# Attention, gated MLP and phase mixing on one core: bias layer by max(w1 L, −b1 ψ), bit-mask float64 conversion, xT at the bottom of its stack

## The chip, the cores and the metric

One core of a Trainium2 chip. The metric is the device time of one execution in microseconds; lower is better. The kernel before takes 879.43 us (median of three runs, 874.92 to 885.33).

## The reference

The output comes out of three layers one after another, for B = 4, S = 576, eight heads of 64:

```python
psi_rel = log1p(|i - j|);  psi_i = log1p(max(i, 1))
h = maximum((psi_rel / psi_i) * w1 + b1, 0)          # S x S x 32
scores = q @ k.T / 8 + (h @ w2)                      # one bias map per head
x = softmax(scores) @ v                              # B x 576 x 512

u, v = split(gelu_tanh(x @ w_in))                    # 512 wide each
v_s = w_sg @ (layer_norm(v) * g_ln) + b_sg
x = x + (u * v_s) @ w_out

theta = x @ w_theta
y = w_tok_r @ (x * cos(theta)) + w_tok_i @ (x * sin(theta))
u = x + y;  out = u + maximum(u @ w_ch, 0)
```

The weights of the second and third layer (w_in, w_out, w_theta, w_tok, w_ch) arrive as float64, two 32-bit words per number, and the kernel makes float32 of them itself. Products of the second and third layer are formed from a high and a low part of each operand.

## The kernel before, in words

The code does not emit instructions where it is written. A recorder (class Rec) takes down every operation with the tiles it reads and writes; plan() then orders them for each engine by a key (set in the code as nc.key) plus a number per tile name from a table SHIFT, chooses the engine where an operation has alternatives with the help of a table BIAS, and emits all of them from one line (379, so every row of the trace has L379). Each engine works through its queue in that order. SBUF pools are stacks: a pool that is opened above another can only use the space once what lay there before is released. Names of tiles in the trace are those in the code; cva... and cvs... are the conversion's two scratch tiles, raw... what it loads.

The stages, in order of build():

- bias_gen: 36 groups of 4 tiles hq of 128 rows (4 query rows by 32 hidden units): hq = max(L·(w1/ψ), −b1) on DVE or relu(L·(w1/ψ) + b1) on ACT (every third group), where L is a sliding window of a table lt of log1p(|i−j|); four 32-row matmuls pb; an eviction bs on ACT or DVE; then a DMA into the bias maps. Beside it v_all is read in 12 pieces for its sum of squares. Everything lies in the pool "start".
- w1_load: pool "wstage". conv64 turns w_in into float32 in 16 chunks of 256 columns (rawwi, cvawi, cvswi, ri); a Square with accumulation gives a power-of-two scale, then wi gets high and low float16 parts. w_sg is read into rs, five tiles, once, and split in the same way (ws, wsr).
- att_pair, 16 times (4 batches by 4 head pairs), 9 tiles each: PE scores s, DVE e = −(s + bias) with its row minimum, ACT exp in place with the row sum, ACT p (high half), POOL or DVE p (low half), a transposing DMA pT<-p, PE px. After nine tiles DVE xf = px/sum, PE transposes it (xq), xT gets its high and low half and is written out (dx). Pool xTp is opened after "wstage" is released. e has 4 buffers (tag "s"), pT 8, xf 1.
- mlp for the batch before runs between the pairs: vp, up, sp on PE; gelu on ACT; layer norm (mv, n) and gates (gg).
- conv_w turns w_out, w_theta, w_tok and w_ch into float32 (wr_...), in halves of 256 or 288 columns, and splits each block (wo, wt, wk, wc).
- s2 multiplies by w_out and adds x (op, xs, x); theta forms tp = x @ w_theta, then rk (rounded tp/2π), rr (rest), sine and cosine by ACT, multiplied with the transposed x (xp) and split into z; ymix forms yp with w_tok; s4 forms cp with w_ch and writes oo.

The low half of every split (p, z, wk, ...) is a TENSOR_TENSOR subtraction that may go to DVE or POOL. In conv64 the steps stand like this:

```python
nc.scalar.activation(a, hi.bitcast(F32), AF.Abs)
nc.scalar.activation(s, hi.bitcast(F32), AF.Sign)
nc.vector.tensor_scalar(a, a, F64_MIN, F64_MAX, op0=ALU.max, op1=ALU.min)
nc.vector.tensor_scalar(ai, ai, 3, 0x40000000, op0=ALU.logical_shift_left, op1=ALU.bitwise_xor)
nc.vector.scalar_tensor_tensor(ai, lo, 29, ai, op0=ALU.logical_shift_right, op1=ALU.bitwise_or)
nc.scalar.activation(a, a, AF.Abs)
self.tt(("vector", "gpsimd"), dst, a, s, ALU.mult)
```

Of the kernel before, what the change touches and what calls it, by code (L numbers as in the profile page):

```python
# [199 lines left out]
def covers(a, b):  # L200
# [23 lines left out]
    ("wr_w_ch", "vector"): 23.7807, ("wr_w_out", "gpsimd"): 12.3712, ("wr_w_out", "vector"): -46.9618,
    ("wr_w_theta", "gpsimd"): -39.3403, ("wr_w_theta", "vector"): 12.8239, ("wr_w_tok", "gpsimd"): -122.2832,
    ("wr_w_tok", "vector"): -39.8631, ("ws", "scalar"): 33.4611, ("ws", "vector"): 72.0963,
    ("wsr", "scalar"): 146.0824, ("wsr", "vector"): 78.6932, ("wt", "gpsimd"): 146.2282,
    ("wt", "vector"): 72.383, ("xT", "scalar"): 34.9432, ("xT", "sync"): -81.3085, ("xT", "vector"): -9.533,
# [1077 lines left out]
```

## Time and profile before

| | |
|---|---|
| median of three runs | 879.43 us (874.92 to 885.33) |
| the profiled execution | 881.56 us, span 879.8 us, mean granted TensorE clock 0.917 |
| busy in the span | PE 762.3 (87%), DVE 629.9 (72%), ACT 520.5 (59%), POOL 298.4 (34%) |
| moved by DMA | 115.52 MB, mean 131 GB/s |

The profile shows one execution. Times are microseconds from the start of the span unless marked ns. PE is TensorE, DVE VectorE, ACT ScalarE, POOL GpSimd; PEclk is the granted clock as a share of 2.4 GHz. In a group's row, the last column is idle time of the engine ahead of these instructions and what ended it.

### The profile page before, as it was taken

How to read it: one execution, taken by the hardware profiler on the slowest of the kernel's cores; microseconds unless marked ns; L12 is line 12 of the kernel's file. 1: busy time of each engine (PE TensorE's matmuls, PEld its weight loads, DVE VectorE, ACT ScalarE, POOL GpSimd, SP SyncE). 2: the span in 40 equal slices, each digit the busy share in tenths (PEclk: the TensorE clock that was granted, in tenths of full speed). 3: DMA queues.
4: the chain of work that ended last, by engine and by line, in shares of the span. 5: the costliest groups of instructions: out<-in, count | busy, mean ns of one | idle time of the engine just before them, and what ended most of it. 6: DMA issues, size and time to landing. Idle time of an engine off the chain costs nothing.

```text
span 879.8 us, 17586 instructions
## 1 busy us (share of the span) xinstructions
PE 762.3 (87%) x6544; PEld 534.8 (61%) x6544; DVE 629.9 (72%) x1475; ACT 520.5 (59%) x1038; POOL 298.4 (34%) x263
## 2 busy tenths in 40 slices
PE   5689778648899889997999976998878999999998
PEld 2234344326454555545654453687757999899998
DVE  5777558869698568986589754997989892763712
ACT  5777567865689447892579713655568671542500
POOL 0011244643567335672547531365433200000000
PEclk9979956557999999999799996999999999999999
DMA  7987689729898299866998396465622210010101
GB/s 227 217 169 172 169 184 192 150 87 192 158 186 154 72 221 179 169 150 133 190 188 151 77 179 159 133 198 173 180 82 64 74 54 1 1 55 1 41 14 54
DMA packets 205734, 115.52 MB, mean 131 GB/s; under 512 B 176593, under 2 KB 176849, under 8 KB 205649
## 3 DMA queue, kind: packets, MB, share of 16 engines
q1 hardware_dynamic: 198192, 101.01, 52.6%
q10 hardware_dynamic: 7456, 13.40, 5.0%
q8 instruction: 51, 0.84, 0.4%
q14 instruction: 35, 0.28, 0.1%
HBM read 47.13 MB, written 14.16 MB: 70 GB/s over the span
## 4 chain that ended last, share of the span: by engine, by line
PE 52%; DVE 17%; DMA 15%; issue 7%; ACT 5%; POOL 3%; SPq 1%; ACTq 0%; DVEq 0%; POOLq 0%
PE yp L379 12%; PE s L379 8%; PE cp L379 6%; DMA pT<-p 6%; PE pb L379 6%; PE sp L379 5%; PE tp L379 4%; PE up L379 4%; PE px L379 4%; PE vp L379 3%; POOL p L379 2%; DVE v L379 2%; DMA vr<-v_all 2%; DVE e L379 2%; DVE cvaw_tok L379 2%
## 5 line engine op out<-in xcount | busy, mean ns | idle before, releaser
L379 POOL TENSOR_TENSOR p<-e,p 128x576 f16<-128x576 f32 x144 | 191.0, 1338 | 183.3 <-ACT p L379 172.5
L379 PE MATMUL s<-kq 64*128 64x288 f32 (+1 forms) x640 | 149.1, 495 | 21.5 <-DVE m L379 21.5
L379 ACT ACTIVATE e<-e,m 128x576 f32<-128x576 f32 x144 | 110.6, 769 | 55.9 <-DVE m L379 44.7
L379 PEld LDWEIGHTS <-pT 128*128 128x128 f16 (+1 forms) x2240 | 86.0, 108 | 69.4 <-issue 30.4
L379 PE MATMUL px<-v,pT 128*128 128x64 f16 (+1 forms) x2240 | 95.4, 204 | 32.6 <-DMA pT<-p 21.9
L379 PE MATMUL yp<-wk,z 128*128 128x288 f32 x864 | 119.4, 297 | 1.5 <-ACT z L379 0.8
L379 DVE CUSTOM_DVE_ANT_0 e<-s,bias 128x576 f32<-128x576 f32 x128 | 94.6, 752 | 35.5 <-PE s L379 18.7
L379 PEld LDWEIGHTS yp<-wk,z 128*128 128x128 f32 x864 | 116.5, 190 | 2.6 <-ACT z L379 1.1
L379 PEld LDWEIGHTS s<-kq 64*128 64x128 f32 (+1 forms) x640 | 71.9, 199 | 65.8 <-DVE m L379 40.3
L379 ACT ACTIVATE p<-e 128x576 f16<-128x576 f32 x144 | 94.0, 674 | 29.7 <-DMA pT<-p 22.2
L379 PE MATMUL pb<-hq,w2s 128*32 128x288 f32 x576 | 69.3, 454 | 14.3 <-DVE bs L379 9.9
L379 PE MATMUL op<-sp_g,wo 128*128 128x288 f32 x384 | 60.8, 311 | 7.6 <-DVE x L379 4.1
L379 PE MATMUL vp<-wi,xT 128*128 128x512 f16 (+1 forms) x240 | 63.4, 397 | 1.4 <-DVE xT L379 1.4
L379 PEld LDWEIGHTS op<-sp_g,wo 128*128 128x128 f32 x384 | 54.4, 194 | 12.4 <-DVE x L379 4.9
L379 PEld LDWEIGHTS pb<-hq,w2s 128*32 128x32 f32 x576 | 28.4, 117 | 52.9 <-DVE bs L379 9.9
L379 PE MATMUL sp<-ws,n 128*128 128x64 f16 (+1 forms) x384 | 57.4, 287 | 0.3 <-DVE n L379 0.2
L379 PE MATMUL up<-xT,wi 128*128 128x64 f16 (+1 forms) x384 | 55.1, 287 | 0.7 <-DVE gtu L379 0.7
L379 ACT ACTIVATE sp_u<-x 128x576 fp32r<-128x576 f32 x16 | 10.8, 684 | 70.8 <-DVE x L379 70.1
L379 PE MATMUL cp<-sp_u,wc 128*128 128x288 f32 x384 | 52.5, 295 | 0.0
L379 PE MATMUL tp<-wt,sp_t 128*128 128x512 f32 x192 | 47.9, 403 | 4.3 <-DVE sp_t L379 2.6
L379 DVE TENSOR_SCALAR hq<-lt,sl,nb 128x576 f32<-128x576 f32 x96 | 49.8, 586 | 2.4 <-PE pb L379 1.6
L379 PEld LDWEIGHTS cp<-sp_u,wc 128*128 128x128 f32 x384 | 51.2, 188 | 0.2
(197 smaller groups left out, 1214.9 us busy)
## 6 DMA issues: line engine op xcount, KB each, us to landing
bias<-bs SPq DMA_DIRECT2D x32, 288.0 KB
kq<-kq SPq DMA_DIRECT2D x10, 576.0 KB
raww_tok<-w_tok SPq DMA_DIRECT2D x18, 288.0 KB
vr<-v_all SPq DMA_DIRECT2D x12, 384.0 KB
xx<-dx SPq DMA_DIRECT2D x16, 288.0 KB
out<-oo SPq DMA_DIRECT2D x16, 288.0 KB
dg<-gg SPq DMA_DIRECT2D x16, 256.0 KB
raw<-vp SPq DMA_DIRECT2D x12, 320.0 KB
```

The lines of the kernel that those rows point to most:

```text
L379: getattr(getattr(self.nc, name), m)(*[res(x) for x in a], **out)
```

## The change

- Bias layer: the division by ψ moves behind the second layer. With ψ > 0, relu(L·w1/ψ + b1) = relu(L·w1 + b1·ψ)/ψ. lt is multiplied by w1 once; hq is max(window, −b1·ψ) with one pointer on DVE, or relu(window + b1·ψ) on ACT; the eviction bs multiplies by 1/ψ (rp, one more pointer). nl, rp are new small tiles; the four matmuls of a half now depend on all four hq of the group. v_all is read in 8 pieces of 1152 columns.
- conv64 has a form with no Sign and no product: absolute value straight into the target, clamp, shift and mask, then the sign bits of the high word are put back by an and/or. The w_in chunks are 512 columns wide and eight; conv_w takes a whole block.
- w_sg is read twice through one buffer rs instead of once into five.
- xTp is opened first, at the bottom of the left stack, and released last. e has 3 buffers, pT 7, xf 2.
- w_theta is scaled by 1/2π at conversion (conv_w's scale), so rr = rk − magic − tp is one operation and Sin takes scale −2π; a subtraction and a second product go.
- SHIFT gets an entry per group of work as well (op.grp, "@a0" is pair 0), and BIAS, SHIFT, LOADF, LOADK, BV, SLACK and YIELD have new numbers.

```diff
@@ plan
-            op.skey = (op.key[0] + SHIFT.get(op.lab, 0.0), op.key[1])
+            op.skey = (op.key[0] + (SHIFT.get(op.lab, 0.0) + SHIFT.get(op.grp, 0.0)), op.key[1])
@@ tables (two of their lines)
-    ("z", "gpsimd"): 22.3176, ("z", "vector"): 16.3112,
+    ("z", "gpsimd"): -58.9563, ("z", "vector"): 12.3072,
@@ conv64
+        if fuse:
+            nc.scalar.activation(dst, hi.bitcast(F32), AF.Abs)
+            nc.vector.tensor_scalar(dst, dst, F64_MIN, F64_MAX, op0=ALU.max, op1=ALU.min)
+            nc.vector.tensor_scalar(di, di, 3, 0x3FFFFFF8, op0=ALU.logical_shift_left, op1=ALU.bitwise_and)
+            nc.vector.scalar_tensor_tensor(di, hi, TOP, di, op0=ALU.bitwise_and, op1=ALU.bitwise_or)
+            nc.vector.scalar_tensor_tensor(di, lo, 29, di, op0=ALU.logical_shift_right, op1=ALU.bitwise_or)
+            return
@@ bias_gen
+        nc.vector.tensor_scalar(nl, sl, b1, -1.0, op0=ALU.mult, op1=ALU.mult)
+        self.th = nc.vector.tensor_scalar(lt, lt, w1, None, op0=ALU.mult)
+        nc.vector.tensor_scalar(sl, sl, b1, None, op0=ALU.mult)
-                    nc.scalar.activation(h, win, AF.Relu, scale=sl[:, Q:Q + 1], bias=b1)
+                    o = nc.scalar.activation(h, win, AF.Relu, bias=sl[:, Q:Q + 1])
-                    nc.vector.tensor_scalar(h, win, sl[:, Q:Q + 1], nb, op0=ALU.mult, op1=ALU.max)
+                    o = nc.vector.tensor_scalar(h, win, nl[:, Q:Q + 1], None, op0=ALU.max)
-            nc.any(("scalar", "activation", (bv, ps[:, :, :SH], AF.Identity), {"bias": add}),
-                   ("vector", "tensor_scalar", (bv, ps[:, :, :SH], add, None), {"op0": ALU.add}))
+            nc.any(("scalar", "activation", (bv, ps[:, :, :SH], AF.Identity), {"bias": add, "scale": rs}),
+                   ("vector", "tensor_scalar", (bv, ps[:, :, :SH], rs, add), {"op0": ALU.mult, "op1": ALU.add}))
@@ w1_load
-            for k in range(8):
-                self.conv64(sp, ri[:, cc, cs], src, 256, f"wi{half}_{k}")
+            for cc in range(4):
+                self.conv64(sp, ri[:, cc], d["w_in"][:, cc, hs], 512, f"wi{half}_{cc}", 2, True)
-        rs = sp.tile([P, 5, S], F32, name="rs")
+            rs = sp.tile([P, S], F32, tag="rs", bufs=1, name=f"ra{st}")
+            rs = sp.tile([P, S], F32, tag="rs", bufs=1, name=f"rs{st}")
@@ att_tile, pair_main
-        s = a.tile([P, S], F32, tag="s", bufs=4, name=f"e{u}")
+        s = a.tile([P, S], F32, tag="s", bufs=3, name=f"e{u}")
-        pT = a.tile([P, 9, P], F16, tag="pT", bufs=8, name=f"pT{u}")
+        pT = a.tile([P, 9, P], F16, tag="pT", bufs=7, name=f"pT{u}")
-        xf = a.tile([P, 4, P], F32, tag="xf", bufs=1, name=f"xf{u}")
+        xf = a.tile([P, 4, P], F32, tag="xf", bufs=2, name=f"xf{u}")
@@ theta
-            nc.scalar.activation(k, ps, AF.Identity, scale=1.0 / (2 * math.pi), bias=self.magic)
-            nc.vector.tensor_scalar(k, k, MAGIC, None, op0=ALU.subtract)
-            nc.vector.scalar_tensor_tensor(r, k, -TWO_PI_HI, ps, op0=ALU.mult, op1=ALU.add)
-            nc.vector.scalar_tensor_tensor(r, k, -TWO_PI_LO, r, op0=ALU.mult, op1=ALU.add)
+            nc.scalar.activation(k, ps, AF.Identity, bias=self.magic)
+            nc.vector.scalar_tensor_tensor(r, k, MAGIC, ps, op0=ALU.subtract, op1=ALU.subtract)
@@ build
+        self.p_x = nc.pool("xTp")
         self.setup()
         self.bias_gen()
...
         self.w1_load()
-        self.p_x = nc.pool("xTp")
         self.p_c1 = nc.pool("c1p")
```

Two places show how the order moves. The first is DVE in the conversion of w_in, about the first xT of the program. wi<-ri is the low half of w_in, bsg the scaling of b_sg, v the split of V for a pair, e a score tile. Before:

```order
L379 SCALAR_TENSOR_TENSOR wi<-ri_1864,fc_wi_136,wi 128x512 x4
L379 TENSOR_SCALAR i2s_131<-ih_134 128x1
L379 COPY v_3_2037<-v_3_2037 64x2x256
L379 TENSOR_SCALAR bsg<-bsg,i2s_131 128x576
L379 TENSOR_SCALAR gsc<-gsc,i2s_131 128x4
L379 COPY v_3_2037<-v_3_2037 64x2x256
L379 SCALAR_TENSOR_TENSOR v_3_2037<-raw_3_1400,fc_v,v_3_2037 128x2x320
L379 TENSOR_SCALAR gts_132<-ih_134 128x1
L379 TENSOR_SCALAR ghs_133<-ih_134 128x1
L379 CAST xT_0_2097<-xq_0_1802 128x512
L379 CAST xT_0_2097<-xq_0_2_2004 128x64
L379 TENSOR_TENSOR xT_0_2097<-xq_0_1802,xT_0_2097 128x512
```

and now:

```order
L384 ISA e_2_2_0_1485,m_2_2_0_1365<-s_2_2_0_1469,biasr 128x576
L384 ISA m_2_2_0_1365 128x1
L384 TENSOR_SCALAR m_2_2_0_1365<-m_2_2_0_1365 128x1
L384 CAST xT_0_170<-xq_0_1492 128x512
L384 SCALAR_TENSOR_TENSOR wi<-ri_1097,fc_wi_146,wi 128x512 x4
L384 ISA e_2_0_0_1531,m_2_0_0_1385<-s_2_0_0_1488,bias_78 128x576
L384 ISA m_2_0_0_1385 128x1
L384 TENSOR_REDUCE ss_sg<-ssb 128x1 x2
L384 TENSOR_SCALAR m_2_0_0_1385<-m_2_0_0_1385 128x1
L384 TENSOR_SCALAR r_2_2_1404<-sr_2_2_1221 128x1
L384 TENSOR_TENSOR xT_0_170<-xq_0_1492,xT_0_170 128x512
L384 TENSOR_SCALAR ri_1562<-ri_1562 128x512 x4
```

gts, ghs, gsc, i2s are small constants of the MLP, m and r of the softmax. The first xT stood behind the last low halves of w_in (x4), the scaling of bsg and a split of v; now its cast stands ahead of the four low halves of the first half of w_in, and the conversion of the second half (ri) follows.

The second place is DVE at the last theta tiles of batch 3 (rk_3 and rr_3 belong to tile 3, the last; oo is an output of batch 2, z the low half). Before:

```order
L379 TENSOR_SCALAR rk_3_10289<-rk_3_10289 128x512
L379 SCALAR_TENSOR_TENSOR rr_3_10296<-rk_3_10289,tp_3_10251 128x512
L379 SCALAR_TENSOR_TENSOR oo_0_9919<-cp_0_10128,x_2_7222 128x576
L379 TENSOR_TENSOR rr_2_10206<-xp_2_10194,rr_2_10206 128x512
L379 SCALAR_TENSOR_TENSOR rr_3_10296<-rk_3_10289,rr_3_10296 128x512
L379 TENSOR_TENSOR rk_2_10213<-xp_2_10194,rk_2_10213 128x512
L379 TENSOR_TENSOR z_3_10192<-rr_2_10206,z_3_10192 128x512
L379 SCALAR_TENSOR_TENSOR oo_1_9958<-cp_1_10227,x_2_7222 128x576
L379 TENSOR_TENSOR z_3_10183<-rk_2_10213,z_3_10183 128x512
```

and now:

```order
L384 SCALAR_TENSOR_TENSOR rr_2_9780<-rk_2_9789,tp_2_9749 128x512
L384 TENSOR_TENSOR rr_2_9780<-xp_2_9767,rr_2_9780 128x512
L384 TENSOR_TENSOR rk_2_9789<-xp_2_9767,rk_2_9789 128x512
L384 SCALAR_TENSOR_TENSOR rr_3_9805<-rk_3_9816,tp_3_9773 128x512
L384 SCALAR_TENSOR_TENSOR oo_0_9459<-cp_0_9669,x_2_7099 128x576
L384 TENSOR_TENSOR rr_3_9805<-xp_3_9797,rr_3_9805 128x512
L384 TENSOR_TENSOR rk_3_9816<-xp_3_9797,rk_3_9816 128x512
L384 SCALAR_TENSOR_TENSOR oo_1_9553<-cp_1_9734,x_2_7099 128x576
```

A theta tile has three DVE rows where it had seven; its two z halves are on POOL, where the last eight stand in one piece:

```order
L384 TENSOR_TENSOR z_3_9682<-rr_0_9421,z_3_9682 128x512
L384 TENSOR_TENSOR z_3_9674<-rk_0_9402,z_3_9674 128x512
L384 TENSOR_TENSOR z_3_9697<-rr_1_9462,z_3_9697 128x512
L384 TENSOR_TENSOR z_3_9690<-rk_1_9491,z_3_9690 128x512
L384 TENSOR_TENSOR z_3_9711<-rr_2_9780,z_3_9711 128x512
L384 TENSOR_TENSOR z_3_9704<-rk_2_9789,z_3_9704 128x512
L384 TENSOR_TENSOR z_3_9725<-rr_3_9805,z_3_9725 128x512
L384 TENSOR_TENSOR z_3_9718<-rk_3_9816,z_3_9718 128x512
```

All 36 z low halves are on POOL now, after none before; on PE these z are followed by 80 cp matmuls and then by the first yp of batch 3 (before, 36 tp, 96 cp and all 216 yp). Evictions bs on DVE go from 18 to 9, and DVE has 1245 rows where it had 1397.

## Rows read from the trace of the kernel before

**Rows 1.** Stretches of the span: us, busy us by engine (x), PEclk, DMA, GB/s.

```profile
0.00:103.00 103.00, 79.77 (x651) 33.97 (x652) 72.75 (x162) 69.42 (x107) 7.32 (x13) 0.93 0.79 188
103.00:185.00 82.00, 56.69 (x375) 33.55 (x371) 58.37 (x172) 64.65 (x163) 43.70 (x40) 0.58 0.78 168
185.00:206.00 21.00, 10.69 (x152) 8.69 (x152) 14.25 (x46) 11.56 (x30) 4.89 (x6) 0.52 0.48 109
206.00:546.00 340.00, 300.91 (x3225) 175.55 (x3226) 252.42 (x692) 214.20 (x429) 178.75 (x149) 0.95 0.81 161
546.00:713.00 167.00, 151.63 (x998) 126.00 (x996) 149.92 (x278) 109.07 (x228) 63.69 (x57) 0.97 0.41 123
713.00:880.00 167.00, 162.58 (x1154) 157.00 (x1152) 82.16 (x129) 51.61 (x84) 0.00 (x0) 1.00 0.08 29
```

**Rows 2.** Chain of waits, 176 to 242: start, us, what.

```profile
...
184.32 0.75 DVE e L379
...
205.52 1.33 DVE xT L379 x3
206.84 0.66 DVE e L379
...
```

**Rows 3.** Timeline of POOL and DVE near 567 and 657: start us, us.

```profile
...
567.13 1.32 POOL L379 TENSOR_TENSOR gg<-gg,gtu 128x512 f32<-128x512 f32 x1 [4.60 <-DVE gg L379]
...
567.23 1.37 DVE L379 TENSOR_SCALAR cvaw_theta<-cvaw_theta 128x256 f32<-128x256 f32 x1
...
569.12 0.48 DVE L379 TENSOR_SCALAR cvaw_theta<-cvaw_theta 128x256 int32<-128x256 int32 x2
...
657.23 0.41 DVE L379 TENSOR_SCALAR rk<-rk 128x512 f32<-128x512 f32 x1
...
```

**Rows 4.** Groups of the run: engine, names, shapes xcount | busy, mean ns.

```profile
L379 DVE TENSOR_SCALAR hq<-lt,sl,nb 128x576 f32<-128x576 f32 x96 | 49.8, 586 | 2.4 <-PE pb L379 1.6 <-DMA lt<-ltab 0.7
...
L379 ACT ACTIVATE hq<-lt,wb,sl 128x576 f32<-128x576 f32 x48 | 38.8, 859 | 3.5 <-DVE m L379 2.1 <-PE s L379 0.8 <-issue 0.5
...
L379 ACT ACTIVATE p<-e 128x576 f16<-128x576 f32 x144 | 94.0, 674 | 29.7 <-DMA pT<-p 22.2 <-DVE v L379 4.8 <-DVE xT L379 2.0
...
L379 DVE TENSOR_SCALAR bs<-pb,cb 128x576 f32<-128x576 f32 x17 | 13.9, 817 | 15.4 <-PE pb L379 9.1 <-DMA bias<-bs 5.6 <-issue 0.6
...
L379 POOL TENSOR_TENSOR p<-e,p 128x576 f16<-128x576 f32 x144 | 191.0, 1338 | 183.3 <-ACT p L379 172.5 <-issue 1.9 <-DMA dx<-xT 1.8
...
L379 PE MATMUL cp<-sp_u,wc 128*128 128x288 f32 x384 | 52.5, 295 | 0.0
...
```

**Rows 5.** Groups of ACT, 103 to 206.

```profile
...
L379 ACT ACTIVATE cvawi<-rawwi 128x256 f32<-128x256 f32 x16 | 6.7, 425 | 4.4 <-DMA rawwi<-w_in 4.3
L379 ACT ACTIVATE cvswi<-rawwi 128x256 f32<-128x256 f32 x16 | 6.7, 417 | 0.0
L379 ACT ACTIVATE wi<-ri 128x256 f16<-128x256 f32 x16 | 6.5, 406 | 1.5 <-POOL ri L379 1.5
L379 ACT ACTIVATE cvawi<-cvawi 128x256 f32<-128x256 f32 x16 | 6.3, 406 | 3.7 <-DVE cvawi L379 3.5
...
```

**Rows 6.** 546 to 713: tiles cvaw_tok, cvaw_theta, z by engine; two DVE groups.

```profile
546.00:713.00 167.00, 25.32 (x54) 15.69 (x36) 19.66 (x18) 0.97 0.41 123
546.00:713.00 167.00, 13.95 (x24) 6.78 (x16) 6.67 (x8) 0.97 0.41 123
546.00:713.00 167.00, 31.65 (x216) 30.26 (x216) 8.47 (x12) 7.47 (x13) 0.97 0.41 123
...
L379 DVE SCALAR_TENSOR_TENSOR rr<-rk,rr 128x512 f32<-128x512 f32 x7 | 5.9, 840 | 0.0
...
L379 DVE TENSOR_SCALAR rk<-rk 128x512 f32<-128x512 f32 x7 | 4.0, 575 | 3.1 <-ACT rk L379 3.1
```

**Rows 7.** Timeline of DVE, 215 to 230: e, first and fifth tile.

```profile
...
218.65 0.76 DVE L379 CUSTOM_DVE_ANT_0 e<-s,bias 128x576 f32<-128x576 f32 x1 [0.29 <-PE s L379]
...
227.75 0.76 DVE L379 CUSTOM_DVE_ANT_0 e<-s,bias 128x576 f32<-128x576 f32 x1 [2.92 <-POOL p L379]
...
```

More of the change, by code (lines that the diff above doesn't have):

```diff
@@ L157, in __init__ @@
         self.done = self.dma = False
-        self.banks, self.table, self.rows, self.lab, self.port = (), None, P, "", [False]
+        self.banks, self.table, self.rows, self.lab, self.grp, self.port = (), None, P, "", "", [False]
 class Pool:
@@ L224 @@
[L224 to L228, printed above, removed]
@@ L253 @@
-    "xp": -331.5337, "xq": 298.6439, "xr": -67.349, "xs": -569.332, "xx": -233.673, "yp": -63.1746,
-    "z": 114.4221, "zb": 275.7247,
-}
-LOADF, LOADK = 1.8093412586188697, 8.575464505639914
-BV = 1.52008187476998
[5 rows of a table added]
+    "@w_ch": 227.6951, "@w_out": 311.7815, "@w_theta": 548.2913, "@w_tok": 311.2367, "@y0": -961.0679,
[3 rows of a table added]
+    "fa_ws": 1498.3734, "fb_v": 321.7078, "fb_wi": -601.6005, "fb_ws": -913.1623, "fc_v": 1005.3392,
+    "fc_wi": -1788.3783, "fc_ws": 365.7335, "fd_v": -467.0455, "fd_wi": -373.7939, "fd_ws": 1003.5365,
@@ L276, in __init__ @@
         self.nc, self.tc = nc, tc
-        self.key, self.seq, self.ops, self.stack, self.last = 0.0, 0, [], {}, {}
+        self.key, self.grp, self.seq, self.ops, self.stack, self.last = 0.0, "", 0, [], {}, {}
         for n in ("vector", "scalar", "gpsimd", "tensor", "sync"):
@@ L729, in bias_gen @@
         self.ld(self.ident, d["ident"])
-        for i in range(12):
-            nc.key = 1.0 + 5 * i
-            vr = st.tile([P, 768], F32, tag="vr", bufs=2, name=f"vr{i}")
-            self.ld(vr, d["v_all"][:, i * 768:(i + 1) * 768], ("sync",))
+        for i in range(8):
+            nc.key = 40.0 + 5 * i
+            vr = st.tile([P, 1152], F32, tag="vr", bufs=2, name=f"vr{i}")
+            self.ld(vr, d["v_all"][:, i * 1152:(i + 1) * 1152], ("sync",))
             nc.scalar.activation(vr, vr, AF.Square, accum_out=self.ss_v[:, i:i + 1])
@@ L777, in w1_load @@
                 nc.vector.tensor_scalar(self.eps4, ts, ts, 4e-6, op0=ALU.mult, op1=ALU.mult)
-            hs = slice(half * 512, half * 512 + 512)
             for cc in range(4):
@@ L783, in w1_load @@
         nc.key = t
-        rs = sp.tile([P, 5, S], F32, name="rs")
-        for st in range(5):
-            self.ld(rs[:, st], d["w_sg"][:, st])
         ssb = c.tile([P, 5], F32, name="ssb")
         for st in range(5):
-            nc.scalar.activation(self.ws[:, 0, st] if st < 4 else self.wsr[:, 0], rs[:, st], AF.Square,
+            rs = sp.tile([P, S], F32, tag="rs", bufs=1, name=f"ra{st}")
+            self.ld(rs, d["w_sg"][:, st])
+            nc.scalar.activation(self.ws[:, 0, st] if st < 4 else self.wsr[:, 0], rs, AF.Square,
                                  accum_out=ssb[:, st:st + 1])
@@ L1074, in conv_w @@
             r = self.p_st.tile([P, S], F32, tag="wst", bufs=2, name=f"wr_{name}{i}")
-            for q in range(2):
-                cs = slice(q * h, (q + 1) * h)
-                self.conv64(self.p_st, r[:, cs], self.d[name][:, i, cs], h, f"{name}{i}_{q}")
-            self.split(w[:, :, i], r[:, :ncol])
+            self.conv64(self.p_st, r[:, :ncol], self.d[name][:, i], ncol, f"{name}{i}", 2, True)
+            if scale is None:
+                self.split(w[:, :, i], r[:, :ncol])
+            else:
+                nc.scalar.activation(w[:, 0, i], r[:, :ncol], AF.Copy, scale=scale)
+                nc.vector.scalar_tensor_tensor(w[:, 1, i], r[:, :ncol], scale, w[:, 0, i].bitcast(F32),
+                                               op0=ALU.mult, op1=ALU.subtract)
     def s2(self, b, key, step):
         nc, st = self.nc, self.p_st
+        nc.grp = f"@o{b}"
         sp = self.sp_tiles(self.p_s2, f"g{b}")
@@ L1217, in build @@
         self.s2(0, t + 15, 3)
-        self.conv_w(self.wt, "w_theta", DM, 4, t + 15, 3)
+        self.conv_w(self.wt, "w_theta", DM, 4, t + 15, 3, 1.0 / TWO_PI)
         self.s2(1, t + 35, 3)
@@ L1221, in build @@
         self.s2(2, t + 55, 3)
-        for q in (self.ps_c, self.ps_x, self.p_c1, self.p_x, self.p_w1):
+        for q in (self.ps_c, self.ps_x, self.p_c1, self.p_w1, self.p_x):
             q.release()
```

131 lines of the change are left out of this document (68 added, 63 removed), and 45 rows, old and new, of tables (BIAS, SHIFT).

## The prediction

> **What bounds the kernel now.** I read the stretches of the span first, then the chain of waits where they look odd, then the groups of single engines there. The chip tells within about ±1% (the three times shown spread that far), so "faster" and "slower" below mean over 1%.
>
> The stretches [rows 1] show five regimes. In 0 to 103 (bias layer) PE is busy 79.77 us, DVE 72.75, ACT 69.42: no engine is full, three share the bound. In 103 to 185 (first attention tiles beside the conversion of w_in) DMA shows 0.78 and ACT 64.65 of 82 us, the fullest compute engine, while PE has 56.69 at a granted clock of 0.58, that is at the 1.2 GHz level almost throughout. In 185 to 206 every engine is half idle. In 206 to 546 (attention with the MLP) PE is busy 300.91 of 340 at 0.95. In 546 to 713 PE has 151.63 of 167 and DVE 149.92; in 713 to 880 PE has 162.58 of 167 at 1.00.
>
> Why 185 to 206 is hollow stands in the chain [rows 2]: a score tile is taken by DVE at 184.32, the next at 206.84, behind three xT casts at 205.52. xT's pool lies above "wstage" on the same stack, so no xT can be written before the w_in and w_sg conversion has let "wstage" go; xf has one buffer, so the next pair's tiles stand still behind it. 22.5 us hold no score tile.
>
> **Term 1, bias layer (0 to 103).** DVE: each of the 96 hq loses one per-partition pointer. A 128x512 TENSOR_SCALAR without pointers took 0.41 us [rows 3], so one of 576 columns about 0.46; hq with two took 586 ns [rows 4], so a pointer is (0.586 − 0.46)/2 = 0.063 us, and 96 of them 6.0. Nine evictions bs leave DVE (18 to 9) at 0.817 [rows 4]: 7.4. The scaling of lt adds one instruction of 1148 columns, about 0.8, ahead of the first hq; DVE 72.75 → 60. ACT: a pointer costs it (859 − 674)/2 = 93 ns (hq with two against p with none [rows 4]); 48 hq with one less are −4.5, nine more bs at about 0.674 + 2 × 0.093 = 0.86 are +7.7, and the 27 now read a scale pointer too; ACT goes to about 74. PE's instructions stay, and PE is the fullest. So DVE's saving is mostly off the path; ACT, loaded more, may become late for the pb tiles. Ends −10 (PE's 23 us of idle time halved) and +5 (ACT's five microseconds, if they all land on the path); I take **−3**, near the engine that is fullest.
>
> **Term 2, 103 to 206.** xT's pool goes to the bottom, so the 22.5 us stall loses its cause: in the new order an xT is cast ahead of the w_in low halves instead of behind everything. What is late next? By ACT: per 256-column chunk it did Abs, Sign, a second Abs and a Square, 6.7 + 6.7 + 6.3 + 6.5 = 26.2 us in all [rows 5]. Now there are 8 chunks of 512 columns with one Abs and one Square: 16 × 0.65 (p, 576 columns, took 0.674) = 10.4. ACT falls from 64.65 + 11.56 = 76.2 to 60.4; at the share it kept in 103 to 185 (64.65/82 = 0.79) that is 76 us instead of 103: −27. By DMA: 82 × 0.78 + 21 × 0.48 = 74 us of busy time stay, and w_sg is now read twice, which adds five loads; 103 to 206 moved 168 × 82 + 109 × 21 = 16.1 MB, five tiles of 128x576 words are 1.5 MB, so DMA needs about 81 us, at 0.85 busy 95 us: −8. The ten w_sg loads go through one buffer, each behind the reader of the one before, and end when "wstage" does, but only the first MLP waits for that now. Ends 0 (all of it is refilled by DMA) and −40 (the time at which ACT is full). I take **−22**, between ACT and DMA, nearer ACT, as 206 to 546 shows DMA at 0.81 beside more tiles per microsecond.
>
> **Term 3, 206 to 546.** No operation is removed here. e loses a buffer (4 to 3), pT one (8 to 7), xf gains one. PE has 39 us of gaps and the order is new. I take **0**, ends −15 (a third of the gaps) and +33 (rival E).
>
> **Term 4, 546 to 713.** DVE and PE are both near full. DVE loses three things. Conversion: w_tok and w_theta cost it 25.32 + 13.95 = 39.3 [rows 6] (their rows give DVE, ACT and POOL; z's PE and PEld first) (w_ch, converted in the same way, is left out). Now a block of 512 columns takes two one-input and two two-input operations, 2 × 0.41 [rows 3] + 2 × 0.70 (as z, 8.47/12 [rows 6]) = 2.2, one of 576 columns 2.5: 4 × 2.2 + 9 × 2.5 = 31.3, so −8.0. Theta: seven TENSOR_SCALAR rk (575 ns) and seven rr<-rk,rr (840) go [rows 6]: −9.9. The low halves z: twelve, 8.47 us [rows 6], go to POOL. DVE: 149.9 − 8.0 − 9.9 − 8.5 = 123.5. Then PE is next: 151.63 × 0.97 (its clock raised to 1) = 147 if never idle; at the share it has in the last stretch (162.58/167) 151. So the stretch goes from 167 to 151 at best: I take **−14**, ends 0 (rival B) and −20.
>
> Cover that may go: POOL is nearly idle here (63.69 of 167) but slow. A two-input operation of 576 columns takes it 1338 ns [rows 4], so one of 512 about 1.2, against 0.7 on DVE, and DVE's own operations pay when POOL works: a 128x256 TENSOR_SCALAR that takes 0.24 in a run of two at 569.12 took 1.37 at 567.23, beside a POOL operation that ran from 567.13 [rows 3]. That is what rival B rests on. The Trainium skill, "Perfetto Trace Analysis", section Optimizing Scalar/DVE Operations, says that GPSIMD and DVE share an SBUF read port, so that moving work from one to the other might not help; the row at 567.23 bears that out, and by it the −8.5 for z would be taken back and term 4 would be about −5.
>
> **Term 5, 713 to 880.** PE is busy 97% at full clock and its instructions stay: 0. The last theta tiles now wait for eight z halves in a row on POOL, 8 × 1.2 = 9.6 us, but 80 cp matmuls stand on PE before the first yp of the last batch. A cp averages 52.5/384 = 0.137 us [rows 4], so these cover 11 us. Ends −2 and +10 (cover gone); **0**.
>
> **Sum** against the profiled execution, 881.56 (span 879.8 and 1.8 around it): −3 − 22 + 0 − 14 + 0 = −39, so 842.6. That execution is 2.1 us above the median of 879.43; I take the 2.1 off: **840.5**.
>
> **Rivals.**
> A (upside): the new order also closes a third of PE's gaps in 206 to 546, −15 to −20: 822. For: POOL and DVE are each idle a quarter of the time or more there. Against: no wait of that stretch is named by the change.
> B: the tail gains nothing. POOL's 36 z halves, 36 × 1.2 = 43 us, and DVE's two-input operations hold each other up, so DVE's saving is eaten. 840.5 + 14 = 854.5. For: the row at 567.23. Against: DVE would have 43 us of slack in 167 to absorb it.
> C: the front gains little, because DMA sets 103 to 206 and the w_sg chain keeps "wstage", and with it the first MLP, late: −4 instead of −22: 858.5. For: DMA 0.78, and every slice before 103 is as full. Against: 185 to 206 has DMA 0.48, so room was left.
> D: the order fits the numbers it was fitted to and not the chip; gains and new gaps cancel: 879.
> E, the other side: the three-deep ring of e. about 136 of the 144 tiles ran in 103 to 546 (8 earlier), 443/136 = 3.26 us a tile; with three buffers that pace holds only while a buffer's life is under 9.8 us. Before, the fifth tile after one at 218.65 got its buffer at 227.75 and waited 2.92 for POOL: a life of 9.1 us with four [rows 7]. From 9.8 us on the ring decides, and each further microsecond of life costs 136/3 = 45 us. At 10.5 us: 136 × 3.5 = 476, +33 in place of −22; with −3 and −14: 881.56 + 16 − 2.1 = 895.5. Against: the bare chain of a tile (e 0.76 [rows 7], an exp of 0.86 as reckoned for bs, p 0.67 and POOL's p 1.34 [rows 4]) is 3.6 us, the rest is waiting, which shortens with a shorter ring. The Trainium skill, "Perfetto Trace Analysis", section Optimization Strategy, reads a bubble that repeats as a sign that buffers ran out; no row here shows that the 2.92 repeats; where it does, one buffer less makes it worse, by that rule.
>
> **How the numbers follow.** Forecast 0.50, A 0.08, B 0.14, C 0.13, D 0.09, E 0.06. Faster: 0.50 + 0.08 + 0.14 + 0.13 = 0.85; within 1%: 0.09; slower: 0.06. The range goes from below A (term 2 at −28, term 3 at −20, term 4 at −14, term 1 at −10: −72, 807) to above C with part of D: 868. Outside lie most of D, E and the best ends. For the forecast and A to C alone, 815 to 860.
>
> **What would show it.** Right: no stretch of 20 us without a score tile between 100 and 210; the attention's tiles 20 us earlier by number; DVE under 127 us in the stretch that answers to 546 to 713, and PE over 0.93 busy in it. Wrong: score tiles waiting for POOL longer than 2 us in a row (E), DVE's mean for z's neighbours and conversions over 1 us (B), the first MLP's start no earlier than before (C), or gaps of PE in 206 to 546 that grew by what was won before (D).

## The result, and the profile after

The changed kernel takes 851.48 us (median of 4, 849.15 to 857.6) against 879.94: a ratio of 0.9686, 95% interval 0.9609 to 0.9763. That is 28 us faster, where 39 were forecast, and inside the range. The rest of this document shows that the sum came that near by luck: two terms gained what was not forecast, two others did not gain what was.

The profiled execution of the changed kernel is the slowest of its four (857.6 us, span 855.8, mean granted clock 0.906). Its stretches, cut near where the same work ends as in [rows 1] (columns as there):

```profile
...
0.00:88.00 88.00, 60.81 (x618) 26.48 (x618) 58.47 (x137) 68.37 (x103) 7.44 (x12) 0.90 0.80 205
88.00:176.00 88.00, 60.25 (x431) 36.09 (x432) 70.45 (x190) 58.78 (x124) 33.03 (x26) 0.55 0.81 194
176.00:206.00 30.00, 27.31 (x306) 18.84 (x305) 22.49 (x71) 18.13 (x37) 13.90 (x11) 0.83 1.03 198
206.00:525.00 319.00, 294.36 (x3087) 168.15 (x3086) 232.69 (x644) 211.14 (x415) 171.37 (x160) 0.95 0.83 161
525.00:690.00 165.00, 149.13 (x980) 128.26 (x978) 134.37 (x194) 79.56 (x131) 60.76 (x37) 0.93 0.38 120
690.00:856.00 166.00, 160.91 (x1135) 155.00 (x1132) 57.30 (x76) 45.09 (x76) 27.34 (x20) 1.00 0.08 28
```

The bias layer now ends at 88 instead of 102 us. The stretch behind it still shows PE at 0.55 of its clock, and DVE, not ACT, is the fullest there (70.45 of 88; ACT fell from 0.79 to 0.67). The hollow of 185 to 206 is gone: from 176 on PE is busy 27.31 of 30. From the first op (w_out) to the end it takes as long as before, although DVE has 36 us less to do there; before first, then the changed kernel:

```profile
...
552.00:880.00 328.00, 308.20 (x2119) 279.81 (x2118) 227.18 (x392) 156.03 (x301) 62.53 (x55) 0.98 0.24 75
```

```profile
...
525.00:856.00 331.00, 310.04 (x2112) 283.25 (x2109) 191.67 (x269) 124.65 (x206) 88.11 (x57) 0.96 0.23 74
```

To see where time was won, I read from each trace when some marks fall: the end of the last pb matmul, the start of the 36th and of the 144th (last) exp, of the first vp (the MLP of batch 0) and of the first op (w_out), and the stretch from there to the end. All later kernels stand in the same table; "order" says whether plan() ran anew or the changed kernel's own order was kept on every engine.

| kernel | order | last pb | 36th exp | first vp | 144th exp | first op | op to end | median us (ratio, interval) |
|---|---|---|---|---|---|---|---|---|
| before | | 101.4 | 208.3 | 218.4 | 513.2 | 550.8 | 329.0 | 879.9 |
| changed | | 87.4 | 195.2 | 198.4 | 497.9 | 523.5 | 332.3 | 851.5 (0.969, 0.961 to 0.976) |
| e1 no grouping | anew | 85.6 | 191.8 | 197.8 | 493.5 | 526.6 | 346.3 | 870.7 (0.985, 0.975 to 0.995) |
| e2 before + grouping | anew | 94.9 | 203.0 | 209.4 | 518.9 | 552.6 | 337.3 | 886.3 (1.005, 1.001 to 1.009) |
| e3 two pointers | kept | 89.7 | 196.7 | 199.8 | 498.5 | 523.4 | 331.3 | 853.8 (0.968, 0.961 to 0.976) |
| e4 z on DVE | kept | 85.7 | 192.1 | 195.1 | 494.4 | 521.5 | 329.5 | 852.3 (0.965, 0.957 to 0.973) |
| e5 xT's pool on top | anew | 88.0 | 188.7 | 237.5 | 507.2 | 532.0 | 344.7 | 878.5 (0.998, 0.994 to 1.002) |
| e6 before + xT at the bottom | anew | 101.2 | 209.1 | 217.9 | 525.0 | 561.1 | 335.9 | 897.2 (1.016, 1.010 to 1.022) |
| e7 18 bs on DVE | kept | 85.1 | 191.5 | 194.6 | 496.0 | 521.6 | 330.4 | 853.3 (0.968, 0.960 to 0.976) |
| e8 four e, one xf | kept | 85.7 | 192.6 | 195.7 | 492.2 | 519.4 | 330.9 | 851.55 (0.965, 0.960 to 0.969) |
| e9 old tables | anew | 97.4 | 206.3 | 204.0 | 530.0 | 555.8 | 343.7 | 902.3 (1.023, 1.017 to 1.029) |
| e10 DVE load at theta | kept | 84.2 | 192.4 | 195.7 | 495.7 | 521.0 | 345.7 | 872.5 (0.991, 0.987 to 0.995) |
| e11 ACT load at w_in | kept | 84.2 | 195.5 | 198.6 | 495.6 | 521.5 | 330.5 | 860.4 (0.976, 0.972 to 0.980) |
| e12 more PE work | kept | 86.4 | 232.3 | 240.0 | 537.0 | 563.2 | 332.3 | 897.5 (1.018, 1.014 to 1.022) |

Each ratio is to the kernel before in the same batch. One of e8's four executions took 2300.36 us; its median and ratio are of the other three. Kernels in one and the same order differ by 3 us in the last pb with nothing changed ahead of it (84.2 to 87.4; e3 and e7, which change the bias layer, left out), so a mark is good to about that. In the first two rows the gain up to the first op is 27.3 us: 14.0 of it in the bias layer, 12.0 between the last exp and the first op. From the first op on there is none.

### The profile page after: what moved, and what is told of

Read it like the earlier page. It is cut to its first block, busy times and chain, and to the rows that moved or that the text cites. A ratio compares the mean times of both kernels' runs of the same rounds, so it can differ in the third digit from the quotient of the medians.

```text
span 855.8 us, 17230 instructions
## 1 busy us (share of the span) xinstructions
PE 752.8 (88%) x6544; PEld 532.8 (62%) x6544; DVE 575.8 (67%) x1308; ACT 481.1 (56%) x882; POOL 313.8 (37%) x266
## 5 line engine op out<-in xcount | busy, mean ns | idle before, releaser
L384 PE MATMUL yp<-wk,z 128*128 128x288 f32 x864 | 117.1, 295 | 1.7 <-DVE x L384 1.0
L384 PE MATMUL px<-v,pT 128*128 128x64 f16 (+1 forms) x2240 | 94.6, 204 | 23.3 <-DMA pT<-p 15.3
L384 PE MATMUL op<-sp_g,wo 128*128 128x288 f32 x384 | 66.4, 329 | 11.3 <-DVE sp_g L384 6.0
L384 PE MATMUL pb<-hq,w2s 128*32 128x288 f32 x576 | 54.5, 487 | 19.3 <-ACT bs L384 13.8
L384 PEld LDWEIGHTS op<-sp_g,wo 128*128 128x128 f32 x384 | 59.6, 211 | 16.2 <-DVE sp_g L384 7.4
L384 DVE TENSOR_TENSOR x<-x,yp 128x576 f32<-128x576 f32 x16 | 12.1, 754 | 74.6 <-PE yp L384 74.6
L384 PE MATMUL sp<-ws,n 128*128 128x64 f16 (+1 forms) x384 | 55.5, 286 | 0.1
L384 DVE TENSOR_SCALAR hq<-lt,nl 128x576 f32<-128x576 f32 x96 | 45.1, 532 | 14.4 <-PE pb L384 14.2
L384 PEld LDWEIGHTS pb<-hq,w2s 128*32 128x32 f32 x576 | 23.0, 125 | 50.0 <-ACT bs L384 22.7
L384 PE MATMUL up<-xT,wi 128*128 128x64 f16 (+1 forms) x384 | 53.2, 287 | 0.2 <-ACT gtu L384 0.2
```

The lines of the kernel that those rows point to most:

```text
L384: getattr(getattr(self.nc, name), m)(*[res(x) for x in a], **out)
```

## The experiments

**e1, e2: the grouping of the pb matmuls.** PE's time for pb fell from 69.3 to 54.5 us, by rows of the two kernels:

```profile
...
L379 PE MATMUL pb<-hq,w2s 128*32 128x288 f32 x576 | 69.3, 454 | 14.3 <-DVE bs L379 9.9 <-ACT hq L379 2.2 <-DVE hq L379 1.6
```

```profile
...
L384 PE MATMUL pb<-hq,w2s 128*32 128x288 f32 x576 | 54.5, 487 | 19.3 <-ACT bs L384 13.8 <-DVE bs L384 3.8 <-DVE hq L384 1.6
...
L384 DVE TENSOR_SCALAR hq<-lt,nl 128x576 f32<-128x576 f32 x96 | 45.1, 532 | 14.4 <-PE pb L384 14.2
...
L384 DVE TENSOR_SCALAR bs<-pb,rp,cb 128x576 f32<-128x576 f32 x9 | 7.9, 872 | 2.9 <-DMA bias<-bs 2.9
```

The mean of one matmul did not fall (454, now 487 ns): busy time counts overlapping matmuls once, so the matmuls of a group ran beside each other more often. The first and the last of a group's 16 PE rows (taken in order of time) start 1.88 us apart on average before, 1.19 in the changed kernel. I first took the added dependencies for the cause. e1 takes them out, e2 adds nothing else to the kernel before:

```diff
-                    for _, o in hs:
-                        nc.dep(x, o)
```

> The changed kernel without the four added dependencies of each pb matmul on all four hq of its group (the order is planned anew with the same tables). Theory G (the bias layer gained 14 us because the matmuls of a group now go out side by side, so that PE's time for pb fell from 69.3 to 54.5 us): the last pb ends 8 to 14 us later than in the changed kernel (87.4 us), near 97 to 101, pb's busy time is back above 64 us, and the whole is 6 to 14 us slower. Rival L (the gain comes from the lighter hq and the nine evictions that left DVE): the last pb stays at 85 to 91 us and the whole moves by less than 4 us.

> The kernel before with nothing but the four dependencies of each pb matmul added (order planned anew with its old tables). Theory G: the last pb ends at 87 to 94 us in place of 101.4, pb's busy time falls below 60 us, and the whole is 5 to 12 us faster than before, if the later stretches keep their length. Rival L: the last pb ends at 98 to 104 us, the whole within 4 us of the kernel before.

Theory G fell in e1: the last pb stays at 85.6, pb at 52.3 us, and a group's rows start 1.10 us apart without the dependencies. Rival L's last pb came, but not its whole (within 4 us). In e2 the same lines do help: pb takes 58.4 us, the last one ends 6.5 us earlier, and yet the whole is not faster. e1's 19 us stem from elsewhere: until the 144th exp it is ahead of the changed kernel, and from the first op on it takes 346 us in place of 332. PE's longest single wait there is 6.8 us for z, where the changed kernel has 0.7, and x costs 8.7 in place of 3.9:

```profile
...
PE op L384 <- DVE x L384: 8.7, 3, 4.8
PE yp L384 <- ACT z L384: 6.8, 1, 6.8
```

Two lines taken out of the bias layer thus cost 14 us more than 400 us later. The whole order was planned anew with tables that fit another program, and DVE and ACT do have another order there; that this makes the 14 us is the reading left, not a run of its own. From here on I kept the changed kernel's order where that could be done: the program is recorded once as it is, planned, and the variant is emitted in that order.

**e3, e7: lighter hq, fewer evictions on DVE.** e3 gives hq a second pointer (a one) again; e7 puts every second bs on DVE.

```diff
-    o = nc.vector.tensor_scalar(h, win, nl[:, Q:Q + 1], None, op0=ALU.max)
+    o = nc.vector.tensor_scalar(h, win, self.one, nl[:, Q:Q + 1], op0=ALU.mult, op1=ALU.max)
```

```diff
+    if op.lab == "bs" and len(op.alts) == 2:
+        op.rec["n"] = op.rec.get("n", 0) + 1
+        return op.rec["n"] % 2
```

> The changed kernel in exactly its own order on every engine, hq alone with a second pointer again (a factor of one), as it had before: DVE 96 x 0.054 us = 5.2 us (586 against 532 ns), ACT 48 x 0.093 = 4.5 us more in the bias layer. Rival L: the last pb ends 4 to 8 us later (91 to 95 us) and the whole is 4 to 8 us slower. Theory G: the last pb moves by 2 us at most, the whole by less than 3 us. In both, hq on DVE has a mean of 580 to 592 ns.

> The changed kernel in its own order, with every second of the 36 evictions bs on DVE (18 as before the change, where the changed kernel has 9). PE's longest waits for pb there are for bs on ACT (13.8 us) against 3.8 for DVE's. Theory C (ACT is what the bias layer now waits for): the last pb ends 2 to 6 us earlier than 87.4. Rival D (nine evictions off DVE are what made the layer shorter): it ends 3 to 10 us later. Whole: the same sign, up to 6 us.

e3: the last pb comes 2.3 us later than in the changed kernel, 3.3 to 5.5 later than in e4, e8 and e10 to e12, and the whole is within noise; hq's mean on DVE is 600 ns, a little over what was expected. So the pointers are worth some 2 to 6 of the 14 us. e7: 18 evictions on DVE cost nothing (85.1), so neither were the nine that left it the gain.

**e9: the old tables on the new program.**

```diff
-    ("z", "gpsimd"): -58.9563, ("z", "vector"): 12.3072,
+    ("z", "gpsimd"): 22.3176, ("z", "vector"): 16.3112,
...
-SLACK = 1.8677521687491392
+SLACK = 0.37452179436210353
```

> The changed kernel with the numbers of the tables of before (BIAS, SHIFT, LOADF, LOADK, BV, SLACK, YIELD), everything else of the change kept. Theory T (a good part of the 28 us is the order, in the bias layer too, where neither the grouping nor the pointers make the difference): the last pb ends after 93 us, DVE has 14 or more of the evictions, the whole is 10 to 30 us slower than the changed kernel. Rival O (the operations taken out make the gain): the last pb ends at 84 to 91 us and the whole is at most 8 us slower.

Theory T holds in the bias layer: the last pb ends at 97.4, ten of the fourteen us are back. The whole is 51 us slower than the changed kernel, far more than the 10 to 30 expected, and 2.3% slower than before. pb's own time stayed low (56.8), but DVE has 24 of the evictions and PE waits for them:

```profile
...
L380 PE MATMUL pb<-hq,w2s 128*32 128x288 f32 x576 | 56.8, 482 | 23.8 <-DVE bs L380 14.6 <-DVE ssv L380 3.7 <-ACT hq L380 2.3
...
L380 DVE TENSOR_SCALAR bs<-pb,rp,cb 128x576 f32<-128x576 f32 x17 | 14.9, 874 | 9.5 <-DMA bias<-bs 9.1 <-PE pb L380 0.4
...
L380 DVE TENSOR_SCALAR bs<-pb,rp,zb 128x576 f32<-128x576 f32 x7 | 6.1, 871 | 0.0
```

The old numbers were never fitted to this program, so this is no measure of what a new fit alone would bring to the old one; that wasn't tried and stays open. It shows that the removed operations bring nothing in this order.

**e5, e6: the place of xT's pool.** e5 opens it above the conversion pool again; e6 moves it in the kernel before (w_sg through one buffer makes the room).

```diff
-        self.p_x = nc.pool("xTp")
         self.setup()
         self.bias_gen()
...
         self.w1_load()
+        self.p_x = nc.pool("xTp")
         self.p_c1 = nc.pool("c1p")
```

```diff
+        self.p_x = nc.pool("xTp")
         self.setup()
         self.bias_gen()
...
         self.w1_load()
-        self.p_x = nc.pool("xTp")
         self.p_c1 = nc.pool("c1p")
...
-        rs = sp.tile([P, 5, S], F32, name="rs")
+            rs = sp.tile([P, S], F32, tag="rs", bufs=1, name=f"ra{st}")
+            rs = sp.tile([P, S], F32, tag="rs", bufs=1, name=f"rs{st}")
```

> The changed kernel with xT's pool opened above the conversion pool again, as before (order planned anew with the same tables). Theory S (the stall of 22 us really went with the move): a stretch of 10 to 25 us without a score tile is back before the 36th exp, the 36th exp is 5 to 20 us later than the 195 us of the changed kernel. Rival W (the stall was paid for by work that had to be done anyway, the conversion on DVE and the tiles behind it, and the move is worth little): the 54th exp and the first vp are within 6 us of 235 and 198 us. The whole is slower by over 8 us by S, within 6 us by W, as far as the later order stays like it is.

> The kernel before with two edits: xT's pool at the bottom, and w_sg read twice through one buffer, which makes the room for it; e, pT, xf, conversion, bias layer, theta and tables as before. Theory S: no 20 us without a score tile, the 54th exp at 259 - 8 to 259 - 22 us, the whole 8 to 20 us faster than before. Rival W: the 54th exp within 6 us of 259, the first vp within 6 us of 218, the whole within 6 us of before.

My step "the stall loses its cause" fell on both sides. In e6 the first xT is written at 169 instead of 205 us and the hollow is still there: from 178 to 207 no score tile, PE busy 11.71 of 29. On the chain DVE's e stands behind the conversion as before. In both kernels PE had that score tile ready long before DVE took it: at 187.3 us at the latest against 206.8 in the kernel before, at 180.9 against 206.9 in e6. What kept it was DVE's queue, not a buffer:

```profile
...
178.00:207.00 29.00, 11.71 (x171) 9.47 (x171) 21.42 (x63) 17.99 (x46) 8.09 (x9) 0.54 0.60 153
```

```profile
...
182.99 3.22 DMA rawwi<-w_in
...
191.73 3.06 DMA rs<-w_sg
...
199.19 1.45 DVE wi L379 x3
...
206.87 0.76 DVE e L379
```

In e5 the first xT waits until 202 and there is no hollow (first row below). What e5 loses is the MLP of batch 0: first vp 39 us later, and then a burst of MLP work in which no score tile runs while PE is full (second row):

```profile
...
185.00:206.00 21.00, 15.21 (x168) 9.86 (x170) 12.26 (x37) 12.23 (x23) 11.70 (x10) 0.74 1.13 220
265.50:295.00 29.50, 27.11 (x326) 16.46 (x325) 20.41 (x48) 10.63 (x19) 8.89 (x10) 1.00 0.26 71
```

At the first op e5 is 8.5 us behind the changed kernel; the other 12 us come after it, where e1 too lost them. So the move is worth at most some 8 us here, the new planning included, and the pool's place made neither the hollow nor its end. The fitted tables did not end it either: in e9, with the old ones, DVE never goes longer than 7.1 us without a score tile between 120 and 240 us, against 21.7 before and 8.4 in the changed kernel. It is the order that plan() makes of the new program; which of that program's edits brings it was not separated, though a second xf is not needed in the changed kernel's order (e8, below, has one and no hollow).

**e11, e12: what paces 88 to 206.** e11 puts a Sign and a second Abs per chunk back on ACT, into a scratch tile; e12 adds six small matmuls behind px for the first 24 tiles.

```diff
+    nc.scalar.activation(sg, raw[:, :, 1].bitcast(F32), AF.Sign)
+    nc.scalar.activation(sg, ri[:, cc], AF.Abs)
```

```diff
+    for _ in range(6):
+        x = nc.tensor.matmul(self.px[:, 3, 0], self.ones, self.ones[:, :D], start=True, stop=True)
```

> The changed kernel in its own order, with a Sign and a second Abs per chunk of w_in put back on ACT, into a scratch tile that nothing reads: 8 x 2 x 0.65 = 10.4 us of ACT between 88 and 206. Theory of the prediction's term 2 (ACT's relief shortens that stretch): the 54th exp 6 to 13 us later than 235.5. Theory V (DVE, whose share of the conversion did not shrink, and DMA set its pace): the 54th exp within 4 us, the whole within 4 us of 851.5.

> The changed kernel in its own order, with six small matmuls behind the px of each of the first 24 tiles, into a part of px that is written over later: PE has more to do where its granted clock is at 0.50 to 0.59 (88 to 176). Theory K (PE at 1.2 GHz paces that stretch): if the granted clock rises above 0.8 there, the 36th exp is 8 to 20 us earlier than 195.2 and the whole 4 to 15 us faster; if the clock stays, the extra 24 x 1.3 us make it 5 to 25 us later. Theory V (DVE and DMA pace it): the 36th exp within 5 us of 195.2 whatever the clock does.

e11 bears out neither theory in full. The 54th exp comes at 236.8 against 235.5 us, less than the 6 to 13 us of term 2's theory. But from the 8th exp to the 54th it takes 144.5 us, where e3, e4, e7, e8, e10 and the changed kernel take 138.0 to 141.0: some 4 of the 10.4 us show there. And the whole is 9 us slower than e8 in the same batch (0.972 to 0.980 against 0.960 to 0.969 of before), where theory V had 4; where that is lost the profiled execution does not show, as it is the fastest of the five (853.86). e12: the clock stayed at its 1.2 GHz level 64 us longer than in the changed kernel, the 36th exp came 37 us later, and the whole took 46 us more, both beyond the 5 to 25 expected:

```profile
...
88.00:176.00 88.00, 75.92 (x502) 58.72 (x504) 52.78 (x149) 45.81 (x99) 25.26 (x19) 0.55 0.76 169
176.00:240.00 64.00, 61.71 (x435) 48.42 (x432) 30.86 (x97) 26.21 (x53) 17.90 (x16) 0.55 0.55 116
```

The price of the added matmuls was reckoned too low: they took PE 55.5 us up to the 36th exp, not 31. PE's idle time took up a part of it (from 88 us to the 36th exp or a little behind, 30 of 118 us idle in the changed kernel, 14 of 152 here), and 37 us came out, with a new hollow of 21.0 us (193 to 215) in which PE is full. Theory V fell for PE's part: PE's work is on the path there. What the stretch would take at 2.4 GHz could not be shown, as the clock did not rise.

**e8: the ring of e.** Four e and one xf, as before.

```diff
-        s = a.tile([P, S], F32, tag="s", bufs=3, name=f"e{u}")
+        s = a.tile([P, S], F32, tag="s", bufs=4, name=f"e{u}")
...
-        xf = a.tile([P, 4, P], F32, tag="xf", bufs=2, name=f"xf{u}")
+        xf = a.tile([P, 4, P], F32, tag="xf", bufs=1, name=f"xf{u}")
```

> The changed kernel in its own order, with e's ring four deep again and, for the room, xf one deep (both as before; one xf moves in the order). Theory R (the three-deep ring costs the attention time, rival E of the prediction in a small form): the 144th exp 5 to 15 us earlier than 498, the whole 4 to 12 us faster than 851.5. Theory N (the ring of three is enough, as PE, DVE and ACT set the pace): the whole within 4 us of 851.5, or a little slower by the one xf.

Theory N: 851.55 us. The 144th exp is 5.7 us earlier than in the changed kernel's profile, but only 2 to 4 us earlier than in e4, e7 and e11, which have the ring of three. Rival E is out, and the rule of the Trainium skill that spoke for it ("Perfetto Trace Analysis", Optimization Strategy: a bubble that repeats may mean that buffers ran out) found no case here: one e more and one xf less changed, together, nothing that can be measured.

**e4, e10: DVE in the last two stretches.** e4 takes the z halves back to DVE; e10 does so too and adds two DVE operations on rr per theta tile.

```diff
+    if op.lab == "z" and len(op.alts) == 2:
+        return 0
```

```diff
+    nc.vector.tensor_scalar(r, r, 1.0, None, op0=ALU.mult)
+    nc.vector.scalar_tensor_tensor(r, r, 0.0, r, op0=ALU.mult, op1=ALU.add)
```

> The changed kernel in its own order, with the 36 low halves z on DVE at the place where POOL had them. Theory P (in the last two stretches PE sets the pace, DVE and POOL have room): the whole moves by less than 3 us, DVE's busy time rises by 36 x 0.70 = 25 us and POOL's falls by 50. Rival B of the prediction (POOL's z and DVE hold each other up and cost the tail what it could have won): 5 to 12 us faster, the last tp and yp earlier by that.

> The changed kernel in its own order, with the z halves on DVE (e4: no difference that could be measured) and two more DVE operations per theta tile, 18 x (0.41 + 0.68) = 20 us, about what the folding of 1/2pi took out; z and these together put 45 us back on DVE from the last score tile on. Theory P (PE sets the pace there and DVE's relief is worth nothing): the whole within 5 us of 851.5, the stretch from the first op to the end 327 to 335 us as in all kernels in this order. Theory of the prediction's term 4 (DVE's relief of 28 us is worth 14): 12 to 25 us slower.

e4: no difference, so rival B is out as far as z goes. The Trainium skill's rule on it ("Perfetto Trace Analysis", Optimizing Scalar/DVE Operations: the two share a read port, so moving work between them might not help) agrees with that outcome, 852.3 against 851.5 us. e10: 21 us slower, and theory P fell as I had put it. The 12 to 25 us of term 4's own theory is what came. These operations stand in a chain (tp, rk, rr, sine, product, z, yp), not beside it, and PE's xp waits for them:

```profile
...
PE xp L386 <- DVE rk L386: 11.0, 9, 1.9
PE op L386 <- DVE x L386: 3.3, 2, 3.0
PE tp L386 <- ACT sp_t L386: 2.0, 1, 2.0
```

PE's waits for rk are 11.0 us in nine places, where the changed kernel has 3.0 in two. Yet the kernel before carried just such operations and was no slower from the first op on (329.0, here 345.7). So they cost 13 us in the changed kernel's order, 16 against e4 (329.5), and were not felt in the old one, which must have had room for them; no run isolates that. A load that is put back into a kept order shows what the operation costs there, not what its removal won.

## Why the prediction was right, and where it was not

The profiled executions differ by 24.0 us (the changed kernel's is its slowest): −14.0 up to the last pb, +0.9 from there to the 36th exp, −14.2 to the first op, +3.3 to the end, where the terms had −3, −22, 0 and −14. The gain of 25 us that was not forecast made good much of the 40 that did not come; that the total lies in the range is luck in that. Of the signs named for "right", the one on the hollow held; the score tiles came not 20 but 10.5 (the 18th), 23.6 (the 54th) and 15.3 us (the 144th) earlier, DVE is at 134.37 us in the fourth term's stretch, not under 127, and PE at 0.90 of it, not over 0.93.

**Term 1, −3, measured −14.** The direction held, the size not, and it lies outside the term's ends (−10 to +5). The step "PE's instructions stay, and PE is the fullest" failed. pb's 69.3 us were no fixed work: they are 54.5 when a group's matmuls start closer together, at a granted clock of 0.93 and 0.90 in this layer. e1, e3 and e7 rule out the grouping lines, the pointers and the evictions as single causes; with the old tables (e9) 10 of the 14 go. What the new tables alone would do to the old program is open.

**Term 2, −22, measured +1 by the 36th exp and −6 at the first vp, beside the bias layer's 14.** The hollow went as forecast, for another reason (e5, e6): neither the pool's place alone nor the single xf held the tiles. The kernel before wrote its second xf at 198.7 us, ahead of the first xT at 205.4. And the stretch's other tiles became slower: from the 8th to the 36th exp it takes 99.4 us, before 101.5, hollow included. ACT, from which I took the gain, paces it in part at most (e11); PE's work counts there too (e12). I had not counted DVE: its share of the w_in conversion did not fall, 23.8 us before, 24.0 now, since it took over the sign from POOL. That DVE sets the pace there is not shown; no run relieved it.

```profile
...
L379 DVE SCALAR_TENSOR_TENSOR cvawi<-rawwi,cvawi 128x256 int32<-128x256 int32 x16 | 8.7, 548 | 0.3
L379 DVE TENSOR_SCALAR cvawi<-cvawi 128x256 int32<-128x256 int32 x16 | 8.1, 514 | 0.2
L379 DVE TENSOR_SCALAR cvawi<-cvawi 128x256 f32<-128x256 f32 x16 | 7.0, 445 | 7.0 <-ACT cvawi L379 6.2 <-POOL p L379 0.8
```

```profile
...
L384 DVE SCALAR_TENSOR_TENSOR ri<-rawwi,ri 128x512 int32<-128x512 int32 x16 | 14.6, 932 | 0.1
...
L384 DVE TENSOR_SCALAR ri<-ri 128x512 int32<-128x512 int32 x8 | 6.1, 776 | 0.0
...
L384 DVE TENSOR_SCALAR ri<-ri 128x512 f32<-128x512 f32 x8 | 3.3, 418 | 1.6 <-ACT ri L384 1.6
```

**Term 3, 0, measured −14.** From the 36th exp to the first op it takes 328.3 us, before 342.5. PE's work is the same and its idle time fell from 37.7 to 24.6 us:

```profile
...
208.30:550.80 342.50, 304.81 (x3240) 176.86 (x3237) 253.88 (x695) 216.42 (x434) 178.04 (x150) 0.95 0.80 161
```

```profile
...
195.20:523.50 328.30, 303.66 (x3174) 173.37 (x3170) 239.71 (x665) 218.00 (x430) 177.74 (x165) 0.95 0.84 163
```

That is the mechanism of rival A, which had a chance of 0.08. Of the 14 us, 12 lie between the last exp and the first op (37.6, now 25.6). It looks as if the earlier start of the first MLP left less of it to do at the end, but e5 speaks against that: its first vp is 39 us later and it has 24.8 there. The cause stays open. The term was within its bounds.

**Term 4, −14, measured 0 or a little worse (+3.3 with term 5).** Here the bound could have been read more closely. PE's waits from the first op to the end, before and after:

```profile
...
PE op L379 <- DVE x L379: 4.1, 5, 1.7
PE tp L379 <- DVE sp_t L379: 2.6, 1, 2.6
PE op L379 <- ACT sp_g L379: 2.4, 2, 2.1
PE xp L379 <- DVE rk L379: 1.8, 3, 1.2
PE tp L379 <- DVE rr L379: 1.7, 1, 1.7
PE op L379 <- DVE sp_g L379: 1.1, 1, 1.1
PE yp L379 <- ACT z L379: 0.8, 1, 0.8
PE yp L379 <- DVE z L379: 0.6, 1, 0.6
PE sp L379 <- DVE n L379: 0.2, 1, 0.2
```

```profile
...
PE op L384 <- DVE sp_g L384: 6.0, 5, 4.0
PE op L384 <- DVE x L384: 3.9, 4, 2.6
PE xp L384 <- DVE rk L384: 3.0, 2, 2.7
PE op L384 <- ACT sp_g L384: 1.1, 2, 0.7
PE yp L384 <- DVE x L384: 1.0, 1, 1.0
PE yp L384 <- ACT z L384: 0.7, 1, 0.7
PE tp L384 <- DVE sr L384: 0.6, 1, 0.6
PE op L384 <- DVE wo L384: 0.2, 1, 0.2
PE up L384 <- ACT gtu L384: 0.2, 1, 0.2
```

They sum to 15.3 and 16.7 us. PE had 308 us of work in 328, and as long as that work stays (310 now), DVE's 36 us less could not shorten the stretch by much more than these waits. Only 4.9 us of the 15.3 stand at rk, rr and z, whose operations the change removes or moves, and 3.7 of the 16.7 still do (rk, z); meanwhile the waits of op for DVE's sp_g grew from 1.1 to 6.0. As the two theta operations cost 13 to 16 us in this order (e10), what their removal won and what the order lost cannot be told apart here; the 0 is what is left of both. The −8.0 for the conversion was wrong besides: w_tok takes DVE 7.3 + 7.1 + 14.5 = 28.9 us now, against 25.3 in [rows 6] and the 9 x 2.5 = 22.5 reckoned. The two operations with the raw words cost what was reckoned (807 ns, for 0.70 x 576/512 = 0.79 us). The one-input ones took 815 and 786 ns on average where 0.46 us was reckoned: 443 to 460 ns in twelve rows, 1421 to 1585 in six, and in all six POOL worked beside them for over three quarters of the time, like the row beside POOL in [rows 3]. That is rival B's mechanism, at the conversion instead of at z. With w_theta (13.95, now 10.8 us) the two stay at 39.7 us, after 39.3:

```profile
...
L384 DVE SCALAR_TENSOR_TENSOR wr_w_tok<-raww_tok,wr_w_tok 128x576 int32<-128x576 int32 x18 | 14.5, 807 | 0.1
...
L384 DVE TENSOR_SCALAR wr_w_tok<-wr_w_tok 128x576 f32<-128x576 f32 x9 | 7.3, 815 | 0.2 <-ACT wr_w_tok L384 0.2
L384 DVE TENSOR_SCALAR wr_w_tok<-wr_w_tok 128x576 int32<-128x576 int32 x9 | 7.1, 786 | 0.1
```

**Term 5, 0.** Held: 166 us for the last stretch, as before.

What rival D said of the order is true as far as e1, e5 and e9 go: it moves more than any single edit; but these tables carried over to the chip, so the change did gain. C's price (−4 in the front) was near what the front gained beside the bias layer, but w_sg's chain, though it now ends 28 us later (206.2), held nothing up: the first vp came at 198.4, and the first sp, which reads ws, at 250.7.

## What to carry to other kernels

A busy time of PE is not a price list: matmuls of a group that start far apart look like more work (69.3 against 54.5 us here), so ask what the same instructions cost where nothing is late. Before pricing a saving on an engine, sum the waits of the engine that bounds the stretch, and among them those at the tiles that the change touches; as long as that engine's busy time stays, that sum is the ceiling. And where a planner orders the queues, a small edit re-plans everything: keep the order fixed to price one operation, and read re-planned variants stage by stage, since their totals moved by up to 51 us here, part of it hundreds of microseconds behind the edit. A load put back at no cost shows that it is off the path there; one that costs shows its price in that order alone.
